# Attention with a gated block on one core: 3-and-2-head exponentials, part of them on VectorE, zero matmuls, re-dealt PSUM buffers and deferred normalisation

**Chip and metric.** One core of one Trainium2 chip. Times are device microseconds (us) of one launch; a time quoted alone is a median.

## The reference

```python
def reference(A_x, A_wqkv, A_wo, B_x, B_w_gate, B_w_up, B_w_down):
    # x: (1, 2048, 640) bf16; 32 heads of 20; gated block 640 -> 1728 -> 640
    x = A_x
    h  = x + attention(layernorm(x), A_wqkv, A_wo)      # softmax(q k^T / sqrt(20)) v, then wo
    h2 = h + ((layernorm(h) @ w_gate) * (layernorm(h) @ w_up)) @ w_down
    return h2
```

There are 32 x 2048 x 2048 exponentials. With 128 keys on the partitions and 512 queries along the free axis, one *head block* is 128 x 512, and there are 2048 of them.

## The kernel before

The queries go in four chunks of 512. Within a chunk come 8 groups of 4 heads, within a group 16 key tiles. One key tile of one group is a *step*; half a step, two heads, is a *unit*: two score matmuls into PSUM (the memory that matmuls write), one exponential over 128 x 1024 on ScalarE, and, once per step, four matmuls with the values. Everything else is *background*: a generator that issues a few matmuls after each unit, up to a budget. During the first chunk the background is the projections ("stage 0"); during each later chunk it is the output projection, second layer norm and gated block of the chunk before. I call the change from one chunk to the next a *seam*. Each engine is taken to run its instructions in the order of issue; the timelines below show it (VectorE stands 4.7 us at one that waits, with work behind it). Profiles write PE for TensorE, PEld for its weight loads, ACT for ScalarE, DVE for VectorE and POOL for GpSimd; *cold* is TensorE at half its clock, *warm* at the full one (a matmul of 320 columns takes 0.267 and 0.133 us there in the trace of before).

```python
    epool = ...bufs=6                                        # exponentials, bf16
    sA   = ctx.enter_context(tc.tile_pool(name="sA",   bufs=3, space=PSUM))   # scores, 128 x 1024
    accp = ctx.enter_context(tc.tile_pool(name="accp", bufs=1, space=PSUM))   # value accumulator
    mp   = ctx.enter_context(tc.tile_pool(name="mp",   bufs=1, space=PSUM))   # all background matmuls
    ...
    def second_stage(qc):                    # background of chunks 1 to 3
        ...
            pg = mp.tile([P, QW], F32, name="pg", tag="m")
            for c in range(KC):
                nc.tensor.matmul(pg[0:M, :], lhsT=wg[:, c, o:o + M], rhs=ln2T[:, c, :], ...)
                yield 220
            gs = p2s.tile([P, QW], F32, name="gs", tag="gs")
            nc.vector.tensor_copy(gs[0:M, :], pg[0:M, :])
            pu = mp.tile([P, QW], F32, name="pu", tag="m")     # same single buffer: waits for the copy
            ...
    def emit_exp(n):
        nc.scalar.activation(E[:], sp[:], ACT.Exp, scale=LN2_ / UNIT)
    ...
    def normalise(qc, g, acc):
        nc.vector.tensor_copy(accS[:], acc[:])
        for j in range(HP):
            nc.sync.dma_start(rs[32 * j:32 * j + 32, :], accS[32 * j + DH:32 * j + DH + 1, :])
        nc.vector.reciprocal(rr[:], rs[:])
        nc.sync.dma_start(rd[:].rearrange("j (p e) -> (j p) e", p=32), rr[:])
        nc.sync.dma_start(rb[:], bass.AP(...))                 # broadcast of the reciprocals
        nc.gpsimd.tensor_tensor(OnT[g][:], accS[:], rb[:], ALU.mult)
    ...
    for n in range(N + LAG):
        if n + LEAD < N:
            emit_S(n + LEAD)                                   # scores, two units ahead
        if n < N:
            emit_exp(n)
        for s in pv_at.get(n, ()):
            emit_PV(s)                                         # values; at a chunk's end: loads, new background
            ...
        advance(440)                                           # background
```

The softmax here doesn't subtract the row's maximum and nothing guards it: scores larger than these inputs give would overflow.

## Time and profile before

| | before |
|---|---|
| time, median (lowest to highest of 16 runs) | 1788.6 (1761.2 to 1806.5) us |
| ScalarE busy with exponentials | 994.9 us |
| ScalarE idle before exponentials | 617.0 us |
| mean granted TensorE clock of the profiled run | 0.59 |

A row of the costliest groups reads: line, engine, operation, tiles, shapes and count; then busy us and mean ns of one; then the us that the engine stood idle just before these instructions, and what ended most of it. The prediction shows the main rows. TensorE's waits in the kernel before (what was waited for: us in total, times, longest):

```profile
PE pg L264 <- DVE hh L275: 45.6, 49, 3.3
...
PE pv L165 <- DVE Vx L170: 22.6, 19, 4.5
PE pu L271 <- DVE gs L268: 21.4, 38, 1.8
PE pk L154 <- DVE qT L160: 19.1, 24, 3.8
PE py L284 <- DVE ot L287: 13.8, 21, 1.9
PE pk L154 <- DVE kT L158: 12.4, 16, 3.3
PE pk L154 <- DVE Vx L170: 12.2, 6, 5.0
```

All of pg, pu, pk, pv and py use the one background buffer. These seven rows add up to 147 us: TensorE may not start the next group before VectorE has emptied that buffer. The rows left out belong to the layer norm (39.8 us) and the seams (34.5 and 26.8 us).

### The profile page before, as it was taken

The numbers are of one execution on the slowest core, as the hardware profiler recorded it, in microseconds if no ns is written. First come the engines' busy times: TensorE is split into PE (matmuls) and PEld (weight loads), VectorE is DVE, ScalarE is ACT, GpSimd is POOL, SyncE is SP. The second block draws the span as 40 slices with busy tenths as digits, with TensorE's granted clock in tenths as the row PEclk, the third lists the DMA queues.
The fourth block names the chain that finished last, engine by engine and source line by source line (L and its number), as shares of the span: only waits on it lengthen the run. The fifth ranks groups of instructions, "written<-read, shape, count | busy, mean of one in ns | idle before, by whom it ended". The sixth has DMA issues, their size and how long they took to land.

```text
span 1787.4 us, 15333 instructions
## 1 busy us (share of the span) xinstructions
PE 1455.9 (81%) x6000; PEld 333.9 (19%) x6000; DVE 261.5 (15%) x512; ACT 1002.9 (56%) x1036; POOL 59.6 (3%) x90
## 2 busy tenths in 40 slices
PE   4678789889956898999958989899778898996677
PEld 1222111111102111221121112211211122111223
DVE  4411111111002111100021111000021110000321
ACT  3235545445854454599944545899644458993000
POOL 1000000000010000000000000000000000000000
PEclk9975655555556555765565555755655558555556
DMA  3000000000004101000011110000102100001110
GB/s 114 0 7 0 7 5 3 7 4 3 7 20 91 36 15 32 14 15 13 7 36 23 28 32 9 20 7 13 36 1 51 32 5 22 9 13 36 30 41 15
DMA packets 60128, 38.33 MB, mean 21 GB/s; under 512 B 17496, under 2 KB 55320, under 8 KB 60056
## 3 DMA queue, kind: packets, MB, share of 16 engines
q1 hardware_dynamic: 59624, 36.37, 7.9%
q8 instruction: 47, 0.77, 0.2%
q10 hardware_dynamic: 432, 0.98, 0.1%
q14 instruction: 25, 0.20, 0.0%
HBM read 34.19 MB, written 2.88 MB: 21 GB/s over the span
## 4 chain that ended last, share of the span: by engine, by line
PE 55%; ACT 18%; DVE 11%; issue 8%; DMA 5%; SPq 2%; POOL 1%; POOLq 0%; DVEq 0%; ACTq 0%
ACT E L335 18%; PE sp L325 14%; PE pk L154 9%; PE pg L264 7%; PE acc L349 7%; PE pu L271 7%; PE py L284 5%; PE pv L165 2%; DVE hh L275 2%; PE po L243 2%; DMA rs<-accS 2%; SPq L359 2%; DVE gs L268 1%; DMA rb<-rd 1%; PE pt L144 1%
## 5 line engine op out<-in xcount | busy, mean ns | idle before, releaser
L335 ACT ACTIVATE E<-sp 128x1024 bf16<-128x1024 f32 x1024 | 994.9, 1292 | 617.0 <-PE sp L325 616.4
L325 PE MATMUL sp<-qT,kT 32*128 32x512 bf16 x2048 | 590.0, 572 | 37.0 <-ACT E L335 5.5
L349 PE MATMUL acc<-E,Vx 128*32 128x512 bf16 x2048 | 302.1, 579 | 0.9 <-ACT E L335 0.6
L325 PEld LDWEIGHTS <-kT 32*128 32x128 bf16 x2048 | 104.1, 98 | 697.5 <-issue 695.9
L154 PE MATMUL pk<-lnT,Wp 128*128 128x512 bf16 x320 | 165.6, 607 | 45.8 <-DVE qT L160 19.1
L264 PE MATMUL pg<-ln2T,wg 128*128 128x512 bf16 (+1 forms) x280 | 143.7, 617 | 59.6 <-DVE hh L275 45.6
L271 PE MATMUL pu<-ln2T,wu 128*128 128x512 bf16 (+1 forms) x280 | 144.1, 618 | 21.4 <-DVE gs L268 21.4
L284 PE MATMUL py<-Wd,hh 128*128 128x320 bf16 x448 | 100.0, 351 | 16.9 <-DVE ot L287 13.8
L243 PE MATMUL po<-wo,On 128*128 128x320 bf16 x256 | 57.5, 362 | 65.4 <-POOL On L368 34.5
L349 PEld LDWEIGHTS <-Vx 128*32 128x32 bf16 x2048 | 57.1, 101 | 210.8 <-issue 210.7
L368 POOL TENSOR_TENSOR On<-accS,rb 128x512 bf16<-128x512 f32 x32 | 40.5, 1266 | 1430.2 <-DMA rb<-rd 1430.2
L356 DVE COPY accS<-acc 128x512 f32<-128x512 f32 x32 | 22.2, 692 | 404.1 <-PE acc L349 404.1
L165 PE MATMUL pv<-Wr,lnT 128*128 128x320 bf16 x160 | 48.0, 417 | 28.9 <-DVE Vx L170 22.6
L268 DVE COPY gs<-pg 128x512 f32<-128x512 f32 (+1 forms) x56 | 38.5, 688 | 208.4 <-PE pg L264 208.4
L275 DVE TENSOR_TENSOR hh<-gs,pu 128x512 bf16<-128x512 f32 (+1 forms) x56 | 38.3, 685 | 203.5 <-PE pu L271 203.5
L144 PE MATMUL pt<-ident,ln 128*128 128x128 bf16 x160 | 25.6, 302 | 52.2 <-DVE ln L133 39.8
L284 PEld LDWEIGHTS <-hh 128*128 128x128 bf16 x448 | 42.4, 107 | 67.8 <-issue 50.2
L271 PEld LDWEIGHTS <-wu 128*128 128x128 bf16 (+1 forms) x280 | 27.4, 117 | 97.8 <-issue 97.8
L243 PEld LDWEIGHTS <-On 128*128 128x128 bf16 x256 | 24.3, 111 | 93.9 <-issue 47.2
L264 PEld LDWEIGHTS <-wg 128*128 128x128 bf16 (+1 forms) x280 | 26.1, 120 | 83.7 <-issue 70.2
L154 PEld LDWEIGHTS <-Wp 128*128 128x128 bf16 x320 | 24.4, 111 | 85.0 <-issue 84.7
L160 DVE TENSOR_SCALAR qT<-pk 128x512 bf16<-128x512 f32 x32 | 22.0, 686 | 122.5 <-PE pk L154 122.5
(32 smaller groups left out, 205.8 us busy)
## 6 DMA issues: line engine op xcount, KB each, us to landing
rb<-rd SPq DMA_DIRECT2D x32, 256.0 KB
wg<-in_B_w_gate_dram SPq DMA_DIRECT2D x24, 320.0 KB, 6.4
wu<-in_B_w_up_dram SPq DMA_DIRECT2D x24, 320.0 KB
out_dram<-ot SPq DMA_DIRECT2D x16, 160.0 KB, 1.8
Wd<-in_B_w_down_dram SPq DMA_DIRECT2D x1, 2080.0 KB, 14.6
rs<-accS SPq DMA_DIRECT2D x128, 2.0 KB, 1.7
x<-in_A_x_dram SPq DMA_DIRECT2D x3, 640.0 KB
Wr<-in_A_wqkv_dram ACTq DMA_DIRECT2D x3, 320.0 KB
```

The lines of the kernel that those rows point to most:

```text
L144: nc.tensor.transpose(pt[:, c, i * P:(i + 1) * P], ln[:, (c0 + c) * P:(c0 + c + 1) * P], ident[:])
L154: nc.tensor.matmul(ps[:], lhsT=Wp[b][c][:, g * P:(g + 1) * P], rhs=lnT[:, c, sl], start=(c == 0), stop=(c == KC - 1))
L165: nc.tensor.matmul(ps[:], lhsT=lnT[:, c, t * P:(t + 1) * P], rhs=Wr[c][:, 2 * D + hf * HD:2 * D + (hf + 1) * HD], start=(c == 0), stop=(c ...
L243: nc.tensor.matmul(ps[:], lhsT=OnT[g][:, tt * P:(tt + 1) * P], rhs=wo[:, g, hsl], start=(g == 0), stop=(g == G - 1))
L264: nc.tensor.matmul(pg[0:M, :], lhsT=wg[:, c, o:o + M], rhs=ln2T[:, c, :], start=(c == 0), stop=(c == KC - 1))
L268: nc.vector.tensor_copy(gs[0:M, :], pg[0:M, :])
L271: nc.tensor.matmul(pu[0:M, :], lhsT=wu[:, c, o:o + M], rhs=ln2T[:, c, :], start=(c == 0), stop=(c == KC - 1))
L275: nc.vector.tensor_tensor(hf_t[0:M, :], gs[0:M, :], pu[0:M, :], ALU.mult)
L284: nc.tensor.matmul(ps[:], lhsT=hh[f][0:K, tt * P:(tt + 1) * P], rhs=Wd[0:K, f, hsl], start=(f == 0), stop=(f == NF - 1))
L325: nc.tensor.matmul(sp[:, i, :], lhsT=kT[g][32 * j:32 * j + 32, kt * P:(kt + 1) * P], rhs=qT[qc][32 * j:32 * j + 32, g, :], start=True, sto ...
L335: nc.scalar.activation(E[:], sp[:], ACT.Exp, scale=LN2_ / UNIT)
L349: nc.tensor.matmul(acc[32 * j:32 * j + 32, :], lhsT=Vx[kt][:, h * VS:h * VS + 32], rhs=E_of.pop((s, j)), start=(kt == 0), stop=(kt == NT - 1))
```

## The change

The intent: fewer and wider exponentials on ScalarE, some moved to VectorE, a second background buffer and zero matmuls to keep TensorE dense, and no stop at the seams. The core of the diff (cut):

```diff
+D_EVERY = 4          # one head block for VectorE every fourth unit, from unit 16
+LEAD, LAG, RATE0, RATE1, IDLE, EXTRA, WAIT_N = 2, 1, 520, 360, 2, 3, 12   # (one line each)
+def plan():          # units of 3 and 2 head blocks in turn; 747 units, 181 blocks for VectorE
...
-    sA = ctx.enter_context(tc.tile_pool(name="sA", bufs=3, space=PSUM))
+    sA = ctx.enter_context(tc.tile_pool(name="sA", bufs=1, space=PSUM))   # tags s3, s2: 3 and 2 heads
     accp = ...
-    mp = ctx.enter_context(tc.tile_pool(name="mp", bufs=1, space=PSUM))
+    mp = ctx.enter_context(tc.tile_pool(name="mp", bufs=2, space=PSUM))
...
+        for g in range(NG0, G):          # zero fills of kT, qT on ScalarE: 18 in all
+                nc.scalar.copy(dst.rearrange("p (c q) -> p c q", q=QW), <zeros, broadcast>)
...
+    def proj_dense(ft, chs, b):          # dense projections, rows scattered by DMA (81)
...
+    def idle_mm(n):
+        for _ in range(n):
+            if acc_t[0] is not None:
+                nc.tensor.matmul(acc_t[0][:], lhsT=zeros[:, 0:P], rhs=zeros[:], start=False, stop=False, ...)
+    def advance(rate):
+        if now[0] < hold[0] or not bg:
+            return idle_mm(IDLE)         # (two ifs)
+        if EXTRA and now[0] % EXTRA == 0:
+            idle_mm(1)
...
+    def emit_SD(b):                      # a head block for VectorE takes a background buffer
+        sp = mp.tile([P, QW], F32, name="sd", tag="m")
+        score(sp[:], b)
+    def emit_D(b, part):                 # four VectorE instructions, spread over three units
+        fx = 512 * sd (int32);  v = (u - 65536) * u, u = low half of fx;  w = QUAD_C * v + fx;  ed = w / 512 (uint16)
...
-        nc.vector.reciprocal(rr[:], rs[:])
-        ... rd, rb, OnT[g] = accS * rb at once
+        def second(): ... reciprocal, rd, rb
+        def third():
+            if qc:
+                need(("Wo", qc - 1))
+            ... on = accS * rb
+        later.setdefault(now[0] + 4, []).append(second)
+        later.setdefault(now[0] + 8, []).append(third)
...
+        yield -WAIT_N                    # output projection waits 12 units after the seam
```

## The prediction

> **What bounds the kernel now.** I read the groups of instructions first, then the slices of the span, then the timeline of a few microseconds, and last the table of stages. The groups:
>
> ```profile
> L335 ACT ACTIVATE E<-sp 128x1024 bf16<-128x1024 f32 x1024 | 994.9, 1292 | 617.0 <-PE sp L325 616.4
> L325 PE MATMUL sp<-qT,kT 32*128 32x512 bf16 x2048 | 590.0, 572 | 37.0 <-ACT E L335 5.5
> L349 PE MATMUL acc<-E,Vx 128*32 128x512 bf16 x2048 | 302.1, 579 | 0.9 <-ACT E L335 0.6
> ```
>
> ScalarE does 1024 exponentials in 995 us and idles 617 us, all of it for score matmuls: TensorE is late. The slices say why:
>
> ```profile
> PE   4678789889956898999958989899778898996677
> ACT  3235545445854454599944545899644458993000
> PEclk9975655555556555765565555755655558555556
> ```
>
> The granted clock is half for most of the span, and PE is 80 to 90% busy because each matmul takes twice as long. The nine in the first slices is not to be believed. Two lines of the timeline, the same 4 matmuls of 320 columns:
>
> ```profile
> 23.61 1.25 PE L165 MATMUL pv<-Wr,lnT 128*128 128x320 bf16 x4
> 548.56 0.72 PE L243 MATMUL po<-wo,On 128*128 128x320 bf16 x4
> ```
>
> The first, where the row claims full clock, runs at half pace (0.267 us a matmul); the second, in a granted stretch, at 0.133. So the kernel is cold almost throughout. The stages:
>
> ```profile
> 128.00:440.00 312.00, 269.44 (x940) 48.86 (x939) 46.80 (x75) 153.38 (x150) 6.33 (x5) 0.53 0.02 5
> 517.00:545.00 28.00, 1.87 (x7) 0.67 (x8) 0.37 (x2) 0.85 (x2) 5.57 (x2) 0.50 0.42 89
> 575.00:733.00 158.00, 136.58 (x462) 24.18 (x463) 22.52 (x35) 76.44 (x75) 2.53 (x2) 0.50 0.11 24
> 774.00:902.00 128.00, 115.40 (x543) 21.85 (x541) 4.73 (x10) 124.33 (x136) 5.06 (x4) 0.50 0.03 9
> 1671.00:1757.00 86.00, 64.17 (x140) 19.86 (x140) 19.31 (x29) 0.00 (x0) 0.00 (x0) 0.50 0.14 36
> ```
>
> (columns: stretch, length, busy time of PE, weight load, DVE, ACT and POOL with counts, clock, DMA). With projections or the gated block beside the attention, a unit of two heads takes about 2.1 us (312 us for 150 exponentials), bound by cold TensorE. Without (774 to 902), ScalarE is 97% busy and sets the pace; exponential starts there lie 0.904 us apart. At 517 both engines stand still for 28 us: the first output projection, in order on PE, waits for wo. After the last exponential (1624 us) there is a tail of 163 us without attention, mostly cold.
>
> [...] granted stretches are multiples of 3.41 us. I worked out the level by counting columns per window from the starts in the timeline, weighted by active rows (a score matmul has 32 of 128). After every cold window of 0.75 or more the clock was granted; those up to 0.73 stayed cold, with one exception at a window's edge; after warm windows it stayed from 0.40 upward and was lost at 0.36 and less. [...] The gated stage reaches 0.72 in its best windows and just misses. [...]
>
> **The change part by part.** (1) Exponentials: units alternate between 3 and 2 heads (747 units, 373 of 3 and 374 of 2), and 181 of the 2048 head blocks go to VectorE as four instructions. ScalarE floor: 373 x (0.051 + 1.280) = 496 us plus 374 x 0.904 = 338 us, 834 us, against 1024 x 0.904 = 926. Gain 92 us if nothing else bound, of which the wider instruction is only 277 x 0.051 = 14. VectorE gets 181 x about 2.5 us (estimate: three at 0.69, one SBUF to SBUF at about 0.45) = 450 us on top of its 262: about 70% of 1000 us.
>
> (2) Clock: 492 matmuls of zeros into the accumulator (two per unit when there is no other work, one every third unit otherwise), a second PSUM buffer for background matmuls, so they no longer wait for each VectorE copy (before: 20.7 + 42.4 us and more on L271, L264), and three-row-group scores. Cold, per two units with the gated block: scores 2 x 0.54, values 1.37 x 0.55, background 3.27 x 0.427 + 0.2, zeros 0.28: 3.7 us, of which weighted columns 0.58 + 0.59 + 1.40 + 0.28 = 2.85, a level of 0.77. That crosses. Warm, it needs only about 0.40; the same sum at half the column time, 1.43 us of 2.23, gives 0.64. I expect warm from about 20 us after the start to the end of attention.
>
> (3) TensorE warm, per unit, from the warm stretches of before (a score group 0.31 us, a value group 0.33, background 0.216 a matmul plus 0.1 a switch): 0.31 + 0.687 x 0.33 + (1.64 x 0.216 + 0.1) + 0.07 = 1.06 us at the later rate, 1.22 at the first rate of 520. ScalarE needs 834 / 747 = 1.117 us. So stage 0 (projections) stays bound by TensorE by a little, the rest becomes bound by ScalarE with 5% slack.
>
> (4) Dense projections save 80 matmuls (240 for 320), about 17 us warm, within stage 0; 86 row-scatter DMAs and 18 zero fills on ScalarE (about 24 us) come with them, mostly where ScalarE waits anyway.
>
> (5) Waits: reciprocal, broadcast and output projection are put off by 4, 8 and 12 units; wo is loaded ahead. The 28 us stop and those of about 13 us at 898 and 1267, and three gaps of about 9 us behind the layer norm, should go: about 80 us. These are included in the per-unit sums below.
>
> (6) Tail: 14 us of normalisation stays (copy 0.7, DMA 1.7, 1.4 and 6.2, multiply 1.3, issues between). Output projection about 14 us partly cold, norm 6, gated matmuls 140: some 12 cold at 0.427 and the rest at 0.216, 33 us; last 112 matmuls 0.135 each, 16; store 4. Sum 87 us, for 163.
>
> Sum: first exponential at 21 us (23.3 before); the first 24 units 45 us (VectorE: 12 tiles of statistics at about 2.6 us, 16 value copies at 0.49, three key copies: 41 us); 163 units at 1.24 = 202; 560 units at 1.117 with 4 to 6% of stalls = 655; tail 87. Together 1010 us. I choose 1015.
>
> **The rivals.** A, the clock stays down: zeros might not count as activity, or VectorE waits might hold windows under 0.74. Then units take 4.3 / 2 = 2.16 us in stage 0 and 1.86 after: 404 + 1042 + 150 = about 1590 us. For it: before, a level of 0.72 was not enough, and 0.77 is near. Against: one good window suffices, since 0.40 holds it; while background lasts (some 158 of 187 units) the zeros hardly matter. If only zeros failed to count, each of three chunks would lose about 0.7 us on 25 to 30 units, near 60 us in all: 1070.
>
> B, VectorE or PSUM becomes the bound: the score block for VectorE takes one of the two background buffers, so the next background group finds the other one still unread and PE, in order, waits 0.7 to 1.5 us; ScalarE has only one unit in hand. For it: VectorE at 70 to 85%, in-order. If it cost 0.3 us per unit on 560 units: 1015 + 130 = about 1145 us. Against: the pieces are spread over three units.
>
> C, no slack at all: ScalarE at its floor with everything hidden: 21 + 30 + 834 + 80 = about 950 us (the first units still lose some).
>
> **Range and chances.** C bounds it below, B above, A has perhaps 4%. I give 945 to 1110 us. Faster by over 2% is near certain: even A is 11% faster, since the stops at the seams and the cold copy waits go in any case. Chances 0.97, 0.02, 0.01.
>
> **What would show it right or wrong.** Right: granted clock near 1.0 in the slices from the second to the last but two; exponential groups at about 1.33 and 0.90 us apart; ScalarE busy over 85% between 270 and 900 us; its idle time in all below 200 us; zeros x492 on PE; no stop of more than 5 us at the three seams. Wrong step 2: clock at half in whole stages. Wrong step 3 or rival B: clock 1.0 but ScalarE idle for scores, with PE waiting for VectorE on the background tiles. Wrong step 6: a tail over 110 us. A slow scatter of keys would show as PE waiting for DMA on scores before 150 us.

Three numbers need their source. ScalarE's 0.051 + 1.280 us for a three-head unit was an assumption when it was written, since the kernel before has exponentials of one width only (904 ns is the commonest distance of their starts); the changed kernel's trace shows it, with 1331 ns as the commonest distance after 1536 elements and 904 after 1024. VectorE's 0.69 us is what the trace of before has for 512 elements from PSUM (L268, 688 ns); the 0.45 had no trace behind it then, and the changed kernel has 0.465 (L544). The levels of the clock are the count in the trace of before, where all 23 complete stretches of the clock's records last whole multiples of 3.41 us (3.41 to 355).

## The result and the profile after

The changed kernel takes 1114.2 us (1110.1 to 1119.5 in 11 runs). A ratio here is the mean time of one kernel's fast runs over that of the other's fast runs of the same rounds, so it isn't quite the ratio of the medians quoted: 0.6275 of before, 95% interval 0.6252 to 0.6298. The predicted time was 1015 us; the result lies 4 us above the range.

The slices of the changed kernel, and its groups:

```profile
ACT  5465878897995799999998799999987999998000
PEclk9668999999998999999898999999998999999689
```

```profile
L512 ACT ACTIVATE E<-sp 128x1536 bf16<-128x1536 f32 x747 | 865.7, 1274 | 125.1 <-PE sp L497 111.4
L497 PE MATMUL sp<-qT,kT 32*128 32x512 bf16 x1867 | 299.0, 392 | 30.4 <-ACT E L512 21.5
L475 PE MATMUL acc<-zeros 128*128 128x512 bf16 x492 | 167.4, 392 | 0.0
L389 PE MATMUL po<-wo,on 128*128 128x320 bf16 x256 | 53.2, 335 | 36.6 <-POOL on L582 27.4
```

The clock is up almost throughout, but for the second to fourth slices and the tail. ScalarE's idle time before exponentials is 125 us in place of 617, but it lies in a few places, where the ACT row dips: the first slices, the middle of stage 0, and the three seams (near 346, 610 and 840 us). So I took the spacing of the exponentials from the trace and set it beside the prediction's own sum:

| term of the sum | predicted us | measured us | difference |
|---|---|---|---|
| first exponential | 21 | 21.5 | +0.5 |
| first 24 units | 45 | 86.0 | +41 |
| next 163 units (rest of stage 0) | 202 | 218 | +16 |
| last 560 units | 655 | 698 | +43 |
| tail | 87 | 89.7 | +3 |
| sum | 1010 | 1113.5 | +104 |

Three stretches hold the whole error. The profile of the changed kernel has a sign of each.

**The first 24 units.** The table of stages, 21 to 110 us, the sum row only (length; busy us of PE, weight load, DVE, ACT, POOL):

```profile
sum 89.00, PE 57.39 PEld 21.17 DVE 43.97 ACT 49.42 POOL 6.63; mean PE 9.57 PEld 3.53 DVE 7.33 ACT 8.24 POOL 1.10
```

VectorE has 44 us of work here, close to the 41 that the prediction counted. But it takes 89 us to do it: no engine is busy for even two thirds of the stretch. The timeline of ScalarE:

```profile
23.79 2.43 ACT L512 ACTIVATE E<-sp 128x1536 bf16<-128x1536 f32 x2
26.12 1.89 ACT L187 COPY kT<-zeros 128x2048 bf16<-128x2048 bf16 x1
27.91 1.99 ACT L187 COPY qT<-zeros 128x512 bf16<-128x512 bf16 x2
...
33.49 2.36 ACT L512 ACTIVATE E<-sp 128x1536 bf16<-128x1536 f32 x2
50.91 1.45 ACT L512 ACTIVATE E<-sp 128x1536 bf16<-128x1536 f32 x1 [15.06 <-PE sp L497]
```

The zero fills stand in ScalarE's queue in bunches of 7.4 us, ahead of exponentials that are ready; then ScalarE waits 15 us.

**The rest of stage 0.** The timeline of VectorE near 150 us:

```profile
150.22 0.69 DVE L539 SCALAR_TENSOR_TENSOR w<-v,fx 128x512 f32<-128x512 f32 x1
155.64 0.25 DVE L571 RECIPROCAL rr<-rs 128x16 f32<-128x16 f32 x1 [4.73 <-DMA rs<-accS]
155.81 0.63 DVE L253 CAST tmp<-pd 128x512 bf16<-128x512 f32 x1
```

The reciprocal waits 4.7 us for its DMA, and the copy behind it, which TensorE needs to get its buffer back, waits with it. The clock falls to half at 156.4 us for 3.4 us.

**The first seam.** The issues on the SP queue:

```profile
336.22 5.13 SPq L629 DMA_DIRECT2D Wd<-in_B_w_down_dram  x1
...
342.10 2.52 SPq L573 DMA_DIRECT2D rd<-rr  x1
353.29 0.60 SPq L575 DMA_DIRECT2D rb<-rd  x1
```

The last group's reciprocals queue up behind the 2 MB of Wd; the broadcast rb follows only at 353, and TensorE stands at the output projection for 13 us. The units 200 to 210 take 26.9 us.

### The profile page after: what moved, and what is told of

Same layout as the page of the kernel before. It is cut to its first block, busy times and chain, and to the rows that moved or that the text cites. A ratio compares the mean times of both kernels' runs of the same rounds, so it can differ in the third digit from the quotient of the medians.

```text
span 1113.5 us, 16694 instructions
## 1 busy us (share of the span) xinstructions
PE 969.5 (87%) x6414; PEld 313.5 (28%) x6414; DVE 703.3 (63%) x1302; ACT 894.1 (80%) x781; POOL 69.6 (6%) x94
## 4 chain that ended last, share of the span: by engine, by line
PE 45%; ACT 28%; DVE 13%; issue 10%; DMA 3%; SPq 2%; POOL 0%; DVEq 0%; ACTq 0%; POOLq 0%
ACT E L512 26%; PE sp L497 11%; PE acc L555 7%; PE pg L417 4%; PE pu L424 4%; PE acc L475 4%; PE py L437 3%; DVE fx L528 3%; PE pd L233 3%; PE po L389 3%; PE pv L275 2%; PE pk L233 2%; DVE st L204 2%; DVE ln L219 1%; DMA rd<-rr 1%
## 5 line engine op out<-in xcount | busy, mean ns | idle before, releaser
L512 ACT ACTIVATE E<-sp 128x1536 bf16<-128x1536 f32 x747 | 865.7, 1274 | 125.1 <-PE sp L497 111.4
L497 PE MATMUL sp<-qT,kT 32*128 32x512 bf16 x1867 | 299.0, 392 | 30.4 <-ACT E L512 21.5
L528 DVE TENSOR_SCALAR fx<-sd 128x512 int32<-128x512 f32 x181 | 125.0, 691 | 193.3 <-PE sd L497 192.9
L555 PE MATMUL acc<-E,Vx 128*32 128x512 bf16 x1867 | 208.8, 399 | 1.3 <-DVE accS L563 1.2
L475 PE MATMUL acc<-zeros 128*128 128x512 bf16 x492 | 167.4, 392 | 0.0
L534 DVE SCALAR_TENSOR_TENSOR v<-fx 128x512 f32<-128x512 uint16 x181 | 129.4, 715 | 4.3
L539 DVE SCALAR_TENSOR_TENSOR w<-v,fx 128x512 f32<-128x512 f32 x181 | 126.2, 697 | 5.8
L544 DVE TENSOR_SCALAR ed<-w 128x512 uint16<-128x512 f32 x181 | 84.2, 465 | 3.9
L497 PE MATMUL sd<-qT,kT 32*128 32x512 bf16 x181 | 70.2, 388 | 9.6 <-DVE tmp L255 3.7
L555 PE MATMUL acc<-ed,Vx 128*32 128x512 bf16 x181 | 71.7, 396 | 0.3 <-DVE accS L563 0.2
```

The lines of the kernel that those rows point to most:

```text
L475: nc.tensor.matmul(acc_t[0][:], lhsT=zeros[:, 0:P], rhs=zeros[:], start=False, stop=False, skip_group_check=True)
L497: nc.tensor.matmul(out, lhsT=kT[g][32 * j:32 * j + 32, kt * P:(kt + 1) * P], rhs=q_of(g, qc)[32 * j:32 * j + 32, :], start=True, stop=True)
L512: nc.scalar.activation(E[:, 0:len(u), :], sp[:, 0:len(u), :], ACT.Exp, scale=LN2_ / UNIT, bias=-BIAS * LN2_ / UNIT)
L528: nc.vector.tensor_scalar_mul(fx[:], S_of.pop(b)[:], 512.0)
L534: nc.vector.scalar_tensor_tensor(v[:], u, -65536.0, u, ALU.add, ALU.mult)
L539: nc.vector.scalar_tensor_tensor(w[:], v[:], QUAD_C, fx[:], ALU.mult, ALU.add)
```

## The experiments

Eighteen kernels ran. All outputs are right. The table at the end of this section has their times.

### 1. From the kernel before: which part wakes the clock?

The prediction put the clock down to three things together: zero matmuls, the second background buffer, and three-head score groups. These runs take the first two one by one.

**b_before_zeros**: the kernel before plus one zero matmul per unit.

```diff
+    zeros = const.tile([P, QW], BF16, name="zeros")   # memset 0
+        idle_mm(1)                                    # into acc, as in the change
         advance(440)
```

> The kernel before plus one matmul of zeros per unit, nothing else. Clock theory: the cold level of the gated stage rises from 0.72 to about 0.77, so it warms and stays warm; the stretches without background are bound by ScalarE either way. Gated and projection units go from 2.1 to about 1.5 us, the seams and the tail stay: 1500 to 1620 us against 1788, mean clock above 0.8. Rival (zeros are work like any other, and the clock is not set by them): each of 1024 units costs about 0.3 to 0.4 us more where PE is the bound, so 1850 to 2100 us at a clock near 0.59.

Measured: 1813.6 us, ratio 1.0128 (1.0081 to 1.0175): a little slower. The mean clock rose to 0.74, and in the stages with background 32 exponentials came per 50 us (1.56 us each, against 2.03 to 2.13 before), as expected. But in the stretches without background the clock stayed at half, as it had been before (0.50 from 774 to 902 us), and there PE is now busy nearly all the time. A stage with background, then one without:

```profile
300.00:350.00 50.00, 41.06 (x214) 10.97 (x217) 9.79 (x15) 32.04 (x32) 1.27 (x1) 0.94 0.01 2
800.00:850.00 50.00, 48.26 (x187) 9.75 (x188) 0.94 (x2) 38.56 (x39) 2.53 (x2) 0.50 0.03 9
```

In the second, 39 exponentials come in 50 us, 1.28 us each, where before they came at 0.904. The zeros gave time in one stage and took it back in the other.

**b3_before_psum**: the kernel before with the buffers re-dealt, nothing else.

```diff
-    sA = ctx.enter_context(tc.tile_pool(name="sA", bufs=3, space=PSUM))
+    sA = ctx.enter_context(tc.tile_pool(name="sA", bufs=2, space=PSUM))
-    mp = ctx.enter_context(tc.tile_pool(name="mp", bufs=1, space=PSUM))
+    mp = ctx.enter_context(tc.tile_pool(name="mp", bufs=3, space=PSUM))
```

> The kernel before with only the PSUM buffers re-dealt (scores' accumulator 3 to 2 buffers... the background accumulator 1 to 3), no zero matmuls. If the background's single buffer is what makes the stages with background slow (TensorE waits 0.6 to 0.8 us for VectorE every fifth matmul), they fall from about 2.04 us per unit towards 1.77 at the slow clock, and to 1.3 to 1.5 if TensorE's density thereby crosses the level at which the clock rises: total 1550 to 1700. If the zeros alone hold the clock up, the time stays at 1760 to 1810.

Measured: 1424 us in its fast run, 1446 to 1452 in three runs that are labelled slow (over 1.5% above the fastest; the profile fell in one of those). Before took 1784 on that chip. So two numbers in the pool declarations are worth 360 us by the fast run, 335 by the medians: about half of the whole change's 674 and more than the expectation allowed. TensorE's waits in this run:

```profile
PE pt L144 <- DVE ln L133: 39.9, 17, 11.1
...
PE po L243 <- POOL On L368: 34.4, 3, 12.0
...
PE po L243 <- DMA wo<-in_A_wo_dram: 27.5, 1, 27.5
PE pv L165 <- DVE Vx L170: 9.1, 4, 3.4
```

Of the 147 us of waits for a copy, the one row left among the eight largest is pv with 9.1 us (the rows left out are waits for ScalarE, 37.4 us, and for a load, 28.8 us). That makes some 138 us of the gain, if a wait saved is time saved; the other 200 I put down to the clock, which no run separates. The table of stages of this run, stage 0 and a gated stretch:

```profile
100.00:240.00 140.00, 139.30 (x832) 37.14 (x830) 41.17 (x68) 130.63 (x136) 5.07 (x4) 1.00 0.03 9
400.00:510.00 110.00, 102.16 (x344) 17.28 (x343) 17.06 (x27) 57.88 (x58) 2.53 (x2) 0.50 0.15 34
```

In stage 0 the clock is fully up, without a zero matmul, and a unit takes 1.03 us (140 / 136) where it took 2.08 (312 / 150, prediction). In the gated stage it stays at half and a unit takes 1.90 (110 / 58), although PE is busy for 102 of the 110 us.

**b4_before_psum_zeros**: the same, plus a zero matmul per unit, but only while background exists.

```diff
+        if bg:
+            idle_mm(1)
```

> The same re-dealt buffers, and one matmul on zeros per unit only while background work exists. If buffers and density together make the gated stages warm, these run at 1.3 to 1.5 us per unit and the stretches without background at 0.904: total 1450 to 1560. If the slow clock stays, TensorE pays for the zeros at half pace: 1750 or more.

Measured: 1429.3 us, ratio 0.8031 (0.7996 to 0.8067). The same gated stretch warms up:

```profile
400.00:530.00 130.00, 110.82 (x595) 32.52 (x595) 28.13 (x50) 82.02 (x81) 3.53 (x3) 0.88 0.14 30
```

Clock 0.88 (0.56 in b3 over the same stretch), and 1.60 us per unit (130 / 81). But stage 0, warm already, now pays: 46 units there take 56.1 us in place of 47.1, because TensorE is the bound (PE is busy for 147.9 us of 70 to 220) and the zeros are work. The sum is a draw with b3's fast run. So the clock is higher with zeros here, and they still earn nothing net.

**a_nozeros**: the changed kernel without any zero matmul.

```diff
-IDLE = 2
-EXTRA = 3
+IDLE = 0
+EXTRA = 0
```

> The changed kernel without its 492 matmuls of zeros. Clock theory[...]: while background work lasts the level is about 0.61 warm, so it stays warm there; where there is none it is about 0.26, so the clock falls, and on the return of background work the cold level is about 0.75, at the edge. So the mean clock falls clearly below 0.94, with half-clock stretches around each of the three seams, and the time is 1125 to 1300 us against 1114. Rival (the zeros only fill otherwise idle PE and take up to 0.22 us each from useful work): clock unchanged, time 1090 to 1114 us.

Measured: 1105.3 us in one fast run, 1124.0 to 1130.0 in three labelled slow; median 1124.1. Mean clock in the profiled run 0.82 (0.94 with zeros). Either they are worth up to 1% or nothing; this run can't tell. What it does tell: the 492 zero matmuls, 167 us of TensorE's time, are not what makes the changed kernel fast. The clock is at half in a stretch where TensorE has time to spare:

```profile
268.00:346.00 78.00, 66.16 (x374) 15.60 (x371) 47.96 (x75) 76.46 (x68) 6.91 (x3) 0.50 0.19 41
```

ScalarE is busy for 76 of these 78 us, so the half clock costs little there.

**h_noD** and **i_noD_mp1**: the changed kernel without exponentials on VectorE, with two and with one background buffer. (With one buffer I expected those score blocks to lock up against the background, which was not run; hence the pair.)

```diff
-D_FROM = 16
+D_FROM = 1 << 20
 # i_noD_mp1 also:
-    mp = ctx.enter_context(tc.tile_pool(name="mp", bufs=2, space=PSUM))
+    mp = ctx.enter_context(tc.tile_pool(name="mp", bufs=1, space=PSUM))
```

> The changed kernel with no exponentials on VectorE: ScalarE gets 181 head blocks more, 181 x 0.427 = 77 us. If ScalarE sets the pace and VectorE's pieces cost nothing elsewhere, 1180 to 1195 us. If VectorE's four-instruction pieces also hold up the background's PSUM buffers (rival B of the prediction, in part), some 20 to 40 us of that come back: 1150 to 1170.

> The same without exponentials on VectorE and with one background PSUM buffer in place of two, zeros kept. If the second buffer is what keeps TensorE dense (and so the clock up, and the units short), this falls back to 1.6 to 2.1 us per unit of two and a half heads where background work exists: 1300 us or more. If the zeros and the three-head groups hold the clock by themselves, TensorE waits about 0.7 us per background group at full clock and the time is 1190 to 1250.

Measured: 1146.2 us with two buffers (ratio 0.6408), 1336.3 with one (two fast runs 1317 and 1331; ratio 0.7387). The second buffer is worth some 175 us by the fast runs in the changed kernel too (190 by the medians, but two of the four runs with one buffer were slow), although the mean clock of the profiled runs hardly differs, 0.95 and 0.93. The rows of the run with one buffer:

```profile
L424 PE MATMUL pu<-ln2T,wu 128*128 128x512 bf16 (+1 forms) x280 | 100.7, 443 | 27.6 <-DVE gs L421 25.7
L417 PE MATMUL pg<-ln2T,wg 128*128 128x512 bf16 (+1 forms) x280 | 102.1, 451 | 22.8 <-DVE hh L428 21.0
```

The waits of the kernel before are back (with two buffers these two rows idle 0.0 and 0.6 us). The tail suffers most: 159 us against 88, with the clock falling there:

```profile
1155.00:1315.00 160.00, 105.90 (x363) 42.19 (x359) 37.78 (x78) 3.06 (x3) 3.65 (x5) 0.62 0.17 38
```

My expectation tied this run to the clock, and that was wrong for the attention: with zeros and wide groups the clock is up there (0.97 from 470 to 570 us), and the other 100 us or so are lost all the same. In the tail's 71 us the waits and the clock are not told apart.

### 2. The three stretches of the table

Each repair is made alone, on the changed kernel.

**c_fills_dma**: the 18 zero fills by DMA.

```diff
-                nc.scalar.copy(dst.rearrange("p (c q) -> p c q", q=QW),
+                nc.sync.dma_start(dst.rearrange("p (c q) -> p c q", q=QW),
```

> The changed kernel with the 18 zero fills of keys and queries done by DMA, not by ScalarE (24 us of ScalarE time). Theory: three of the fill groups (7.4, 7.4 and 3.7 us) stand in ScalarE's queue ahead of exponentials in the first 24 units, and PE waits 12.7 us in sum for those; so 8 to 14 us less than 1114, and the first 24 units take 72 to 79 us for 86. Rival (ScalarE waits there for scores anyway, the chain of layer norm on VectorE sets the pace): within 4 us of 1114.

Measured: 1105.9 us, ratio 0.6179 against 0.6275. The first 24 units take 76.4 us in place of 86.0; all else is unchanged. As expected.

**g_interleave**: the values of each tile projected right after its transpose, in place of four transposes, then keys, then four tiles of values.

```diff
                 yield from transposed(lns.pop(t), lnT_dst(t), nc.vector.tensor_copy)
+                yield from proj_v(t, 0)
             yield from proj_pad(0, ch, 1)
             done.add(("K", 0, ch))
-            for t in range(ch * TPC, (ch + 1) * TPC):
-                yield from proj_v(t, 0)
```

> The changed kernel with each value projection put directly behind the transpose of its tile in the first stage, in place of four transposes, the keys, then four value projections. Theory: in the first 24 units VectorE (47% busy) and PE (60%) work in turns, so mixing them takes 12 to 25 us off the first 24 units (86 us) and as much off 1114. Rival (VectorE's chain of 2.37 us per tile is the bound and PE's turn is hidden in it, or the fills on ScalarE set it): less than 6 us.

Measured: 1111.3 us. The first 24 units take 90.8 us, longer than before. The theory that the order makes VectorE and TensorE take turns here is not borne out: it forecast 12 to 25 us less.

**j_ln_ahead**: the layer norm of each chunk's first two tiles done while the values of the chunk before are projected.

```diff
             for t in range(ch * TPC, (ch + 1) * TPC):
                 yield from proj_v(t, 0)
+                if t % TPC < 2:
+                    stat(t + 6)      # statistics
+                    app(t + 5)       # normalise
```

> The changed kernel with the layer norm of each chunk's first two tiles done on VectorE while TensorE still projects the values of the chunk before. If the first 24 units are long (86 us) because VectorE's norm chain and TensorE's projections alternate, 10 to 14 us of them go, total about 1100 to 1105. If the slow clock sets these phases, less than 4 us go.

Measured: 1115.4 us, first 24 units 85.2. Nothing, alone. It does work once the fills are gone (below).

**d_wd_late**: the loads of Wd moved behind those that the first output projection waits for.

```diff
         load_w(0)
         load_w(1)
+        if qc == 0:
+            nc.sync.dma_start(Wd[...], ...)    # both loads, from the seam to here
```

> The changed kernel with the 2 MB load of Wd put behind the loads that the first output projection waits for. If that order on the queue is the cause of the 13 us stop near 346 us, the units 200 to 210 take 12 to 14 us in place of 26.9 and the total falls by 10 to 13 us, to about 1101 to 1104. If the normalisation's own round trip is slow whatever stands ahead of it, the total stays within 3 us of 1114.

Measured: 1109.3 us, ratio 0.6224. Units 200 to 210 take 19.9 us in place of 26.9, not the 12 to 14 expected: half of the stop.

**e_norm_late**: reciprocal, multiplication and output projection queued 7, 11 and 15 units late in place of 4, 8 and 12.

```diff
-WAIT_N = 12
+WAIT_N = 15
-        later.setdefault(now[0] + 4, []).append(second)
-        later.setdefault(now[0] + 8, []).append(third)
+        later.setdefault(now[0] + 7, []).append(second)
+        later.setdefault(now[0] + 11, []).append(third)
```

> The changed kernel with the reciprocal and the normalisation queued 7 and 11 units after the row sums' transfer in place of the shorter distances. If VectorE's idle 4.3 to 4.7 us in its own queue, behind a reciprocal that waits for its data, is what stops TensorE and drops the clock near 152 and 250 us, these stops vanish and the total falls by 5 to 12 us. If they are only moved, the total stays within 3 us of 1114.

Measured: 1104.5 us, ratio 0.6198. The rest of stage 0 falls from 218 to 208 us, and VectorE's idle time before the reciprocal from 20.4 to 5.1 us. The clock in 130 to 185 us goes from 0.97 to 1.00. As expected.

**f_no_burst**: the last multiplication is put off by one unit, as often as needed, where it had forced the rest of the former output projection out.

```diff
-            if qc:
-                need(("Wo", qc - 1))
+            if qc and ("Wo", qc - 1) not in done:
+                later.setdefault(now[0] + 1, []).append(third)
+                return
```

> The changed kernel, but the last multiply of a group's normalisation waits for its buffer by being queued again one unit later, and no longer forces the rest of the former chunk's output projection out at once. If that burst is what stretches the units 394 to 410 (29.6 us where 18 are due) and 590 to 600 (20 us where 11.5 are due), about 10 us go: 1102 to 1106. If VectorE's norm burst and the two background buffers set these seams anyway, less than 4 us.

Measured: 1113.4 us. Units 394 to 410 go from 29.6 to 26.0 us, 590 to 600 from 19.7 to 15.1, but the units after each lose most of it again (394 to 440: 63.2 us against 65.3; 590 to 640: 67.1 against 66.8). The burst was not what these two seams cost.

**k_all**: c, d, e, f and j together.

> All of these repairs at once: zero fills by DMA, Wd's load put back, the normalisation queued later, the layer norm ahead, and the last multiply waiting for its buffer without forcing the output projection's rest. If the single gains (8, 5, 10, about 10, about 10 us) lie in different stretches they add up: 1065 to 1080 us. If they take each other's place, 1085 to 1100.

Measured: 1066.9 us, ratio 0.5951 (0.5916 to 0.5986). The gains add up, and more: 47 us by the medians, where the five alone gave 22 (58 and 51 by the ratios). The first 24 units take 67.6 us (76.4 with the fills gone alone; of the other repairs only the norm done ahead acts so early, so it is worth 9 us now), the rest of stage 0 208, units 200 to 210 take 12.9 (14.0 less; alone, d took 7.0 off this seam and e 4.4), the last 560 units 681.

### 3. What is left: the second and third seam, and VectorE's exponentials

Without exponentials on VectorE the changed kernel had lost only 32 us (medians 1146.2 and 1114.2; 24 by the ratios), where ScalarE's arithmetic says 72 units x 1.117 = 80 us. So they give back some 50 us somewhere. Runs on the repaired kernel:

**l_all_noD** (none on VectorE), **n_all_d3** (233 blocks in place of 181) and **m_all_noextra** (no zeros beside background):

```diff
 # l_all_noD
-D_FROM = 16
+D_FROM = 1 << 20
 # n_all_d3
-D_EVERY = 4
+D_EVERY = 3
 # m_all_noextra
-EXTRA = 3
+EXTRA = 0
```

> The kernel with all repairs, without exponentials on VectorE. In the unrepaired kernel taking them away cost 32 us of the 80 that ScalarE's arithmetic gives (72 units x 1.117). If they collide with the queue order and the late reciprocal that are now repaired, they are worth more here, 45 to 70 us: 1112 to 1137. If they give back their 50 us by holding VectorE and a background buffer in any stage, the difference stays 25 to 40 us: 1092 to 1107.

> The kernel with all repairs and a head block for VectorE in every third unit in place of every fourth: about 60 blocks more, 60 x 0.427 = 26 us less for ScalarE, 60 x 2.6 = 155 us more for VectorE (then at some 80%). If ScalarE still sets the pace, 1045 to 1055. If VectorE's pieces and TensorE's load set it, 1067 to 1095.

> The kernel with all repairs, without the one zero matmul in every third unit that runs beside background work (those in units without background stay). If TensorE's load is the bound there, some 150 x 0.21 us = 30 us of its work go and the time falls by 5 to 15 us: 1052 to 1062. If the clock is lost in a stage for it, 1080 or more.

Measured: without these exponentials 1093.3 us (ratio 0.6149), with a third more of them 1077.8 (0.6061), against 1066.9 (0.5951). So 181 of them are worth 26 us by the medians, 35 by the ratios, of the 80, and 233 are worse than 181. Without the zeros beside background 1062.4 us (0.5969): no difference that the intervals show.

The trace of k_all says how they cost. The second seam, timeline of TensorE and then of VectorE:

```profile
566.62 0.39 PE L514 MATMUL sp<-qT,kT 32*128 32x512 bf16 x3 [0.16 <-ACT E L529]
568.70 0.58 PE L514 MATMUL sd<-qT,kT 32*128 32x512 bf16 x1 [1.68 <-DVE ln2T L227]
569.21 0.62 PE L572 MATMUL acc<-E,Vx 128*32 128x512 bf16 x4
```

```profile
567.64 0.61 DVE L219 TENSOR_SCALAR ln<-h,mv,rstd 128x640 bf16<-128x640 f32 x1
568.17 0.48 DVE L227 COPY ln2T<-pt 128x640 bf16<-128x640 bf16 x1
569.32 0.69 DVE L545 TENSOR_SCALAR fx<-sd 128x512 int32<-128x512 f32 x1 [0.67 <-PE sd L514]
```

Both background buffers are full, one of them with transposes that wait in VectorE's queue behind the layer norm. The score block for VectorE (sd) needs a buffer, and TensorE, in order, stands for 1.7 us until the copy. The matmuls after it take 0.6 us in place of 0.39, from 568.7 us to 578.5 (the clock is 0.87 in 550 to 575 us and 0.93 in 575 to 600), and TensorE becomes the bound. A wait of 1.7 us is followed by ten at half clock.

**o_all_noD_seams**: none of these exponentials in some 55 units after each change of chunk; 140 blocks, 763 units.

```diff
-        if n >= D_FROM and n % D_EVERY == 0 and len(left) > 4 * HP:
+        if (n >= D_FROM and n % D_EVERY == 0 and len(left) > 4 * HP
+                and not (left[0][0] >= G * NT and 4 <= left[0][0] % (G * NT) < 42)):
```

> The kernel with all repairs, with no exponentials on VectorE in some 55 units after each change of chunk (140 blocks in place of 181; 763 units). ScalarE gets 16 units x 1.1175 = 18 us more. The seams of the kernel with all repairs are some 39 us longer than ScalarE's arithmetic, those of its twin without exponentials on VectorE almost nothing. If the collision at the seams is the cost, 1042 to 1055 us; if the cost is spread over all stages, 1067 to 1085.

Measured: 1055.3 us, ratio 0.5912 (0.5880 to 0.5943). ScalarE has 16 units more and the kernel is 12 us faster by the medians. By the ratios it is 7, and their intervals overlap, so the traces must decide. The second seam in both, first k_all, then this one:

```profile
548.00:624.00 76.00, 68.27 (x458) 20.40 (x454) 54.78 (x110) 65.80 (x57) 5.08 (x6) 0.91 0.20 41
```

```profile
539.00:604.00 65.00, 61.68 (x441) 20.72 (x438) 23.65 (x57) 64.66 (x58) 6.10 (x7) 1.00 0.20 44
```

The same 57 and 58 exponentials take 76 and 65 us; the clock is 0.91 and 1.00; ScalarE is idle for 10 us and for less than one. In l_all_noD, without any of these exponentials, 58 take 64 us there, at clock 1.00. Over all after stage 0, k_all took 681 us where ScalarE alone needs 626 (560 x 1.1175); this one takes 664 where 639 are needed. The stalls fall from 8.9% to 3.9%. So 25 to 30 us of the 45 to 54 that these exponentials gave back lie in the collision at the seams.

**p_all_rate0**: the same with the background's rate in stage 0 lowered.

```diff
-RATE0 = 520
+RATE0 = 420
```

> The same, and the background's rate in the first chunk lowered from 520 to 420 per unit, so that it lasts to the end of that chunk in place of leaving some 50 units with zeros alone. If TensorE is the bound there only because the work is handed out too early, 8 to 15 us less than the kernel beside it; if the first groups' deadlines force the projections out anyway, no gain within 4 us.

Measured: 1067.6 us, 12 us slower. Stage 0 in both, first this run, then o_all_noD_seams, over the same number of exponentials but one:

```profile
128.00:198.00 70.00, 63.73 (x385) 18.09 (x382) 40.97 (x72) 55.12 (x47) 2.54 (x2) 0.84 0.10 24
```

```profile
120.00:184.00 64.00, 60.12 (x408) 18.72 (x405) 43.55 (x77) 56.45 (x48) 2.84 (x2) 1.00 0.14 32
```

With fewer background matmuls per unit the clock falls to 0.84 here, and TensorE comes later although it has less to do. This stretch holds 6 of the 12 us; 7 more lie in the first 24 units (73.2 us against 66.3). That the lower density is the cause is my reading; the two runs show only that they go together.

### All runs

| kernel | from | median us | ratio to before |
|---|---|---|---|
| before | | 1788.6 | 1 |
| b_before_zeros | before | 1813.6 | 1.0128 |
| b3_before_psum | before | 1448.4 (fast run 1424.1) | none (one fast run) |
| b4_before_psum_zeros | before | 1429.3 | 0.8031 |
| changed kernel | | 1114.2 | 0.6275 |
| a_nozeros | changed | 1124.1 (fast run 1105.3) | none (one fast run) |
| h_noD | changed | 1146.2 | 0.6408 |
| i_noD_mp1 | changed | 1336.3 | 0.7387 |
| c_fills_dma | changed | 1105.9 | 0.6179 |
| g_interleave | changed | 1111.3 | 0.6199 |
| j_ln_ahead | changed | 1115.4 | 0.6224 |
| d_wd_late | changed | 1109.3 | 0.6224 |
| e_norm_late | changed | 1104.5 | 0.6198 |
| f_no_burst | changed | 1113.4 | 0.6267 |
| k_all | changed | 1066.9 | 0.5951 |
| l_all_noD | k_all | 1093.3 | 0.6149 |
| m_all_noextra | k_all | 1062.4 | 0.5969 |
| n_all_d3 | k_all | 1077.8 | 0.6061 |
| o_all_noD_seams | k_all | 1055.3 | 0.5912 |
| p_all_rate0 | o | 1067.6 | 0.5985 |

The kernel before itself shifts by up to 1% (1778 to 1793 us), so a difference of 0.005 between ratios is not much. That holds for g and j above all, whose ratios are low while their medians are those of the changed kernel.

## Why the prediction was right or wrong

**Direction and cause: right, as far as taken apart.** A cold TensorE that also waited bound the kernel, and one run shows that half of the gain comes with the buffers that free it (b3). The clock rose and fell much as step 2 said, if less sharply. I counted again, in pieces of 3.41 us, at whose ends alone the clock changes in these two traces: the columns of each matmul, weighted by active rows, the four matmuls of a value group as one, at the times that the traces have for 512 columns (0.427 us cold, 0.216 warm). These are counts in two traces, not limits of the hardware (in before, pieces of up to 0.76 stayed cold where others of 0.71 and 0.74 were followed by the full clock; a share of 1.03 shows how exact the count is):

| share of columns in the piece | before | changed kernel |
|---|---|---|
| cold, full clock next | 0.71 to 0.97 (11 pieces) | 0.77 to 1.00 (14) |
| cold, half clock next | up to 0.76 (423) | up to 0.80 (23) |
| warm, full clock next | 0.41 to 0.73 (47) | 0.42 to 1.03 (268) |
| warm, half clock next | up to 0.36 (11) | up to 0.38 (14) |

With one background buffer stage 0 is cold (clock 0.53 from 128 to 440 us, before), with three it is at full clock (1.00 from 100 to 240 us, b3); with zeros and wide units, one buffer too held 0.97 in a stretch with background (i_noD_mp1, 470 to 570 us). In k_all a gap of 1.7 us, with shorter ones before it, came just before ten us at half clock (568.7 to 578.5 us).

**Step 2, within that: right in sum, wrong in weight.** It named the zeros first. They are worth about 1% or nothing (a_nozeros, m_all_noextra, b4 against b3) and cost 1.3% in the kernel before (b_before_zeros). The second buffer was the part that mattered. "If only zeros failed to count ... 1070" had no counterpart: the clock is lower without them (0.82 for 0.94 in the mean, a_nozeros), but where it is, TensorE need not be late (from 268 to 346 us ScalarE is busy for 76 of 78).

**Step 3: the unit times were right where nothing interfered.** Without background beside them, units follow at 1.11 to 1.16 us (changed kernel, 780 to 803, 270 to 330 and 555 to 590 us); ScalarE's 1.117 holds: most starts lie 1.33 to 1.35 us apart after 1536 elements and 0.904 after 1024, as assumed.

**The first term failed: "the first 24 units 45 us (VectorE ...: 41 us)".** VectorE's work was sized rightly (44 us measured); the overlap was not. The prediction took the larger of the engines' times, as if VectorE could work all through, but the stretch took 86 us with no engine busy for two thirds of it. Step 2 expected the clock up from about 20 us, and it is up for longer than 7 us only from 98.4 us. 18 fills on ScalarE were placed "mostly where ScalarE waits anyway" (step 4); they stood ahead of exponentials and cost 10 us (c). The norm chain is 9 us more (k_all after c), and nothing alone (j). VectorE's exponentials, which begin with unit 16, are 5 to 6 us: without them the stretch takes 80.9 us (h_noD, for 86.0) and 61.6 (l_all_noD, for 67.6). Some 17 us of the term are not resolved (61.6 against 45). That there VectorE and a cold TensorE take turns, so that their times add, is argued from the table of stages, not shown by a run; g_interleave, meant to mix them, did not help.

**The last term failed: "560 units at 1.117 with 4 to 6% of stalls".** Measured were 11.6% (698 against 626). Step 5 said that the stops "should go"; the first seam kept 13 us, from Wd's place in the queue and the normalisation's distance together (d 7.0, e 4.4, both and the rest 14.0 in k_all). The larger part of what is left is rival B, at the seams. The prediction gave it 0.3 us per unit over 560 units, as a second buffer taken away everywhere; it happens only where layer norm, output projection and these exponentials meet on VectorE, and at the second seam it costs about ten us, the clock being lost with it. With that cured, the stalls are 3.9% (o_all_noD_seams). Four to six per cent was a fair number for a kernel without these faults.

**Step 1 failed by what it counted as free.** 181 head blocks on VectorE save 77 to 80 us of ScalarE and cost most of that elsewhere: 24 to 35 us are left. VectorE's own price was right (0.69, 0.71, 0.70 and 0.47 us, 2.57 in sum, for 2.5); the queue was the trouble, not the sum.

**The middle term, 202 for 218,** was the reciprocal waiting in VectorE's queue, 10 us (e); the rest of stage 0 stays bound by TensorE. **The tail** (87, 89.7) and the first exponential were right.

**Sums and signs.** Some figures of the prediction do not come out as written: rival C's terms add up to 965 us, not 950; rival B's 0.3 us on 560 units is 168 us, not 130; the scattered rows are 81 DMAs, not 86. Of its signs, ScalarE's share from 270 to 900 us (92%), its idle time (125 us) and the 492 zeros came true; full clock from the second slice on (0.6, 0.6 and 0.8 in the second to fourth) and no stop over 5 us at a seam (13.0) did not.

**Open.** From b4 (1429) to the changed kernel (1114) lie the wider units, the moved exponentials, the deferred normalisation and output projection (which let wo load first) and the dense projections; I did not take these apart, save for the moved exponentials (24 to 35 us). TensorE's waits in b3 (27.5 us for wo, 34.4 for On, 39.9 for the layer norm) suggest that the seams and layer norms are about 100 of it, which no run shows.

## What to carry to other kernels

When TensorE runs at half clock, look first for what makes it wait in short pieces, such as a PSUM buffer that VectorE must empty (147 us of waits here). More buffers removed most of those waits here, and the clock of stage 0 was higher with them (0.53 before, 1.00 in b3); zero matmuls raised the clock here too (0.56 to 0.88 in the gated stretch, b3 and b4), but being work themselves they earned nothing that the runs show. Before work is called hidden on an engine with time to spare, look at what stands behind it in that engine's queue and which buffer it holds: an average of 63% busy says nothing of the seam where three users meet. When several small repairs each give 5 to 10 us or nothing, try them together: the norm done ahead gave nothing here until the fills had gone.
